# One 64x64-mode stretch per step for the transposed-attention products, x loaded by another queue, and a new head and tail, in a windowed-attention backward kernel

## The chip, the cores and the metric

One core of one Trainium2 chip. The metric is the device time of that core in microseconds (us); the kernel before takes 2076.82 us (median of 3 runs, 2076.24 to 2077.89). Engines: PE (TensorE matmul), PEld (its weight loads), DVE (VectorE), ACT (ScalarE), POOL (GpSimd), SP (the queue that issues most transfers). "SPq" is SP's queue at work issuing.

## The reference

Windowed self-attention with windows of 8x8 pixels on a 256x256 image with 384 channels, and its gradient. All inputs are bfloat16. The outputs are the forward result and the gradients of x, wqkv and wo.

```python
def _fwd_reference(x, wqkv, wo):          # x: 1,256,256,384
    # xw: 1024 windows of 64 tokens x 384
    qkv = xw @ wqkv
    q, k, v = qkv[..., :C], qkv[..., C:2*C], qkv[..., 2*C:]
    p = softmax(einsum('bqc,bkc->bqk', q, k) * C**-0.5)
    o = einsum('bqk,bkc->bqc', p, v) @ wo
    return o                               # back in image order
def reference(x, wqkv, wo, grad_out):
    out, vjp = jax.vjp(_fwd_reference, x, wqkv, wo)
    return (out, *vjp(grad_out))
```

## The kernel before

The kernel handles a "quad" of four 128-row tiles (two windows each) in a step; 128 quads, so 128 full steps and some for filling and draining. It works with the products A = Wq Wk^T and B = Wv Wo and their transposes, so q, k and v are never formed. A step has products that use the whole 128x128 array (projections `proj`, `wgrad`, `outs`, `dxs`) and products on one window's 64 rows (`scores`, `md`, `attn`, `turn_p`). `md` and `attn` run on 64x64 quarters of the array.

All products go to the eight 512-column float32 banks of PSUM (`PS[:, bank, :]`), and DVE or ACT has to empty a bank (`ev`) before the next user writes there. The parts that matter here:

```python
def load(n):                                   # all loads on SP
    for t in range(4):
        SP.dma_start(out=X[...], in_=img(x, n, t))
        SP.dma_start(out=DO[...], in_=img(grad_out, n, t))

def proj(n, a, banks, engs):                   # 128x128 products, 512 columns
    for mo in range(CK):                       # CK = 3
        o = PS[:, banks[mo], :]
        ...                                    # three products each
        ev(engs[mo], YHT[:, n % NYH, a, mo, :], o)

def md(n):                                     # 64x64 quarters
    for m in range(CK):
        ...                                    # 16 products into banks 2m, 2m+1
        for w in range(2):                     # bank 2m by DVE, 2m+1 by ACT, into MD[:, m]
            ev(DVE if w == 0 else ACT, dst, PS[:, 2 * m + w, :]...)

def outs(n, t0, b0, eng):                      # reads MD[:, 0] first
    for i in range(2):
        for m in range(CK):
            mm(PS[:, b0 + i, 0:C], MD[:, m, t0 + i, 2:4, :]..., B_sb[:, m, :], m == 0, m == CK - 1)
    ev(eng, OS[...], PS[:, b0:b0 + 2, 0:C])

def attn(n, t, bvw, bdx): ...                  # 64x64: VW pieces to two banks, dx pieces to a third

def step(n):                                   # T = n, S = n+1, A = n+2
    load(n + 4); turn_in(n + 3)                # turn_in: DMA transposes XT, DOT on SP
    scores(S); chain1(S)                       # chain: softmax and its gradient, DVE/ACT/POOL
    md(T)
    wgrad(g, k0)
    chain2(S); chain3(S)
    outs(T, 0, 0, ACT); outs(T, 2, 2, DVE); outs_st(T)
    proj(A, 0, (4, 5, 0), (ACT, DVE, ACT)); turn_yh(A, 0)
    wgrad(g, k0 + 1)
    attn(T, 0, 2, 4); attn_ev(T, 0, 2, DVE); attn(T, 1, 0, 5); attn_ev(T, 1, 0, ACT)   # 64x64 stretch 1
    dxs(T, 0, 4, ACT); dxs_st(T, 0)
    proj(A, 1, (2, 3, 1), (DVE, ACT, DVE)); turn_yh(A, 1)
    turn_p(S); turn_p_ev(S)
    attn(T, 2, 2, 4); ...; attn(T, 3, 0, 5); ...                                        # 64x64 stretch 2
    dxs(T, 2, 4, ACT); dxs_st(T, 2)
```
(conditions for the first and last steps cut)

Of the kernel before, what the change touches and what calls it, by code (L numbers as in the profile page):

```python
# [16 lines left out]
def kernel(  # L17
# [13 lines left out]
    P = 128  # L31
# [13 lines left out]
    PS = pp.tile([P, 8, 512], F32, name="PS")  # L45
    X = sb.tile([P, NX * 4, C], BF16, name="X")
# [42 lines left out]
    def load(n):  # L89
        for t in range(4):  # L90
            SP.dma_start(out=X[:, (n % NX) * 4 + t, :], in_=img(x, n, t))  # L91
            SP.dma_start(out=DO[:, (n % ND) * 4 + t, :], in_=img(grad_out, n, t))  # L92

    def turn_in(n):
        xs = X[:, (n % NX) * 4:(n % NX) * 4 + 4, :].rearrange("p t c -> p (t c)")
        SP.dma_start_transpose(out=XT[:, n % NXT, :, :], in_=xs)  # L96
        ds = DO[:, (n % ND) * 4:(n % ND) * 4 + 4, :].rearrange("p t c -> p (t c)")
        SP.dma_start_transpose(out=DOT[:, n % NDT, :, :], in_=ds)  # L98
# [5 lines left out]
    def proj(n, a, banks, engs):  # L104
        wgt = A_sb if a == 0 else BT_sb
        src = (XT[:, n % NXT] if a == 0 else DOT[:, n % NDT]).rearrange("p (t m) k -> p m t k", m=CK)
        for mo in range(CK):
            o = PS[:, banks[mo], :]
            for m in range(CK):
                mm(o.rearrange("p (t k) -> p t k", t=4), wgt[:, m, mo * P:(mo + 1) * P], src[:, m, :, :],  # L110
                   m == 0, m == CK - 1)
            ev(engs[mo], YHT[:, n % NYH, a, mo, :], o)
# [31 lines left out]
    def turn_p(n):  # L144
        bb = PS[:, 6, :].bitcast(BF16)
        for t in range(4):
            for a in range(2):
                for w in range(2):
                    r = slice(64 * w, 64 * w + 64)
                    PE.transpose(bb[r, t * P + a * 64:t * P + a * 64 + 64], PB[r, n % 2, a, t, :], ident[r, r])  # L150

    def turn_p_ev(n):
        ev(DVE, TT[:, n % 2].rearrange("p t a k -> p (t a k)"), PS[:, 6, :].bitcast(BF16)[:, 0:512])

    def md(n):
        for m in range(CK):
# [22 lines left out]
    def attn(n, t, bvw, bdx):  # L179
        xs, ds, vw = (n % NX) * 4 + t, (n % ND) * 4 + t, (n % NVW) * 4 + t  # L180
        for a in range(2):
            src = X[:, xs, :] if a == 0 else DO[:, ds, :]
            yh = YH[:, n % NTOK, a, :, :].rearrange("p (m t) k -> p t m k", m=CK)[:, t]
            for cr in range(2):
                for w in range(2):
                    r = slice(64 * w, 64 * w + 64)
                    o = 64 * (w if cr == 0 else 1 - w)
                    if cr == 0:
                        mm(PS[o:o + 64, bvw + a, 0:C], PB[r, n % 2, a, t, :], src[r, :], True, True)
                    else:  # L190
                        mm(PS[o:o + 64, bdx, 0:C].rearrange("p (m k) -> p m k", m=CK), PB[r, n % 2, a, t, :],
                           yh[r], a == 0, False)

    def attn_ev(n, t, bvw, eng):
        ev(eng, VW[:, (n % NVW) * 4 + t, :, :], PS[:, bvw:bvw + 2, 0:C])

    def dxs(n, t0, b0, eng):
        for i in range(2):
            for m in range(CK):
                mm(PS[:, b0 + i, 0:C], MD[:, m, t0 + i, 0:2, :].rearrange("p a k -> p (a k)"), AT_sb[:, m, :],  # L200
                   False, m == CK - 1)
        ev(eng, DXS[:, n % 2, t0:t0 + 2, :], PS[:, b0:b0 + 2, 0:C])
# [6 lines left out]
    def wgrad(g, k):  # L209
# [3 lines left out]
        for i, (q, t) in enumerate(tiles):  # L213
            mm(PS[:, 7, 0:C], X[:, (q % NX) * 4 + t, ma * P:(ma + 1) * P], VW[:, (q % NVW) * 4 + t, which, :],
               i == 0, i == len(tiles) - 1)
        if g == 0:
            DVE.tensor_copy(out=ACC[:, k, :], in_=PS[:, 7, 0:C])
        else:
            DVE.tensor_tensor(out=ACC[:, k, :], in0=PS[:, 7, 0:C], in1=ACC[:, k, :], op=ALU.add)  # L219

    with tc.manual_schedule():

        wT = VW[:].rearrange("p a b c -> p (a b c)")[:, 0:JK * C].rearrange("p (j c) -> p j c", j=JK)
        wo_sb = VW[:].rearrange("p a b c -> p (a b c)")[:, JK * C:(JK + CK) * C].rearrange("p (m c) -> p m c", m=CK)
        for m in range(CK):
            SP.dma_start(out=w_sb[:, m, :], in_=wqkv[m * P:(m + 1) * P, :])
        ACT.dma_start(out=wo_sb[:], in_=wo.rearrange("(m p) n -> p m n", p=P))
        make_identity(nc, ident[:])
        load(0)
        for m in range(CK):  # L230
            SP.dma_start_transpose(out=wT[:, :, m * P:(m + 1) * P], in_=w_sb[:, m, :])  # L231
        for m in range(CK):
            SP.dma_start_transpose(out=woT_sb[:, :, m * P:(m + 1) * P], in_=wo_sb[:, m, :])  # L233
        k = 0
        for dst, lt, r0, sc in ((A_sb, wT[:, 0:CK], wT[:, CK:2 * CK], True),
                                (AT_sb, wT[:, CK:2 * CK], wT[:, 0:CK], True),
                                (B_sb, wT[:, 2 * CK:3 * CK], wo_sb, False),
                                (BT_sb, wo_sb, wT[:, 2 * CK:3 * CK], False)):
            for mo in range(CK):
                o = PS[:, k % 8, 0:C]  # L240
                for m in range(CK):
                    mm(o, lt[:, m, mo * P:(mo + 1) * P], r0[:, m, :], m == 0, m == CK - 1)
                if sc:
                    ACT.activation(out=dst[:, mo, :], in_=o, func=ACTF.Copy, scale=scale)
                else:
                    DVE.tensor_copy(out=dst[:, mo, :], in_=o)
                k += 1

        def step(n):
            T, S, A = n, n + 1, n + 2  # L250
            doT, doS, doA = 0 <= T < NQ, 0 <= S < NQ, 0 <= A < NQ
            g, k0 = n // GQ - 1, 2 * (n % GQ)
            doF = 0 <= g < NG
            if 0 < n + 4 < NQ:
                load(n + 4)
            if 0 <= n + 3 < NQ:
                turn_in(n + 3)
            if doS:
                scores(S)
                chain1(S)  # L260
            if doT:
                md(T)
            if doF:
                wgrad(g, k0)
            if doS:
                chain2(S)
                chain3(S)
            if doT:
                outs(T, 0, 0, ACT)
                outs(T, 2, 2, DVE)  # L270
                outs_st(T)
            if doA:
                proj(A, 0, (4, 5, 0), (ACT, DVE, ACT))
                turn_yh(A, 0)
            if doF:
                wgrad(g, k0 + 1)
            if doT:
                attn(T, 0, 2, 4)
                attn_ev(T, 0, 2, DVE)
                attn(T, 1, 0, 5)  # L280
                attn_ev(T, 1, 0, ACT)
                dxs(T, 0, 4, ACT)
                dxs_st(T, 0)
            if doA:
                proj(A, 1, (2, 3, 1), (DVE, ACT, DVE))
                turn_yh(A, 1)
            if doS:
                turn_p(S)
                turn_p_ev(S)
            if doT:  # L290
                attn(T, 2, 2, 4)
                attn_ev(T, 2, 2, ACT)
                attn(T, 3, 0, 5)
                attn_ev(T, 3, 0, DVE)
                dxs(T, 2, 4, ACT)
                dxs_st(T, 2)

        for n in range(-3, GQ * NG + GQ):
            step(n)


        GF = YHT[:, 0].rearrange("p a m t -> p (a m t)")[:, 0:6 * C].rearrange("p (k c) -> p k c", k=6)
        GFT = YHT[:, 1].rearrange("p a m t -> p (a m t)")[:, 0:6 * C].rearrange("p (k c) -> p k c", k=6)
        for k in range(6):
            ev(DVE if k < 3 else ACT, GF[:, k, :], ACC[:, k, :])
        for h in range(2):
            for mb in range(CK):
# [3 lines left out]
                ev(DVE if h == 0 else ACT, GFT[:, h * CK + mb, :], pt[:, 0:C])  # L311
        dw = VW[:].rearrange("p a b c -> p (a b c)")[:, 0:CK * J].rearrange("p (m j) -> p m j", m=CK)
        dwo = VW[:].rearrange("p a b c -> p (a b c)")[:, CK * J:CK * J + CK * C].rearrange("p (m j) -> p m j", m=CK)
        k = 0
        for ma in range(CK):
            for col, lt, rr, r0 in ((0, GF[:, 0:CK], w_sb, C), (C, GFT[:, 0:CK], w_sb, 0), (2 * C, GFT[:, CK:], woT_sb, 0)):
                o = PS[:, k % 8, 0:C]
                for mb in range(CK):
                    mm(o, lt[:, mb, ma * P:(ma + 1) * P], rr[:, mb, r0:r0 + C], mb == 0, mb == CK - 1)
                if col < 2 * C:  # L320
# [42 lines left out]
```

## Time and profile before

| | before |
|---|---|
| time, median us | 2076.82 |
| span of the profiled run, us | 2072.7 |
| PE busy | 98% |
| first `md` begins at, us | 43.42 |
| usual period of a step, us | 15.66 |
| last `md` to the end, us | 42.7 |

The period is the distance between the starts of successive `md` groups on PE.

From the page of before, two lines: busy times, and the shares in the chain of work that ended last.

```profile
PE 2029.9 (98%) x26970; PEld 1149.4 (55%) x26970; DVE 1358.6 (66%) x2452; ACT 985.1 (48%) x1555; POOL 1012.9 (49%) x1798
...
PE 96%; DMA 2%; SPq 2%; DVE 0%; ACT 0%; issue 0%; DVEq 0%
```

PE is the bound, so a saving has to come out of PE's own sequence. Here is one step of before in PE's timeline (start, length, engine, line, operation, tiles, shapes, count). Matmuls are pipelined and their ends are modelled, so a group's length overlaps the next group: read the distances between starts.

```profile
1015.20 0.95 PE L73 MATMUL PS<-XT,YHT 128*64 128x64 bf16 x48
...
1016.87 2.12 PE L73 MATMUL PS<-VW,X 128*128 128x384 bf16 x12
1018.83 2.11 PE L73 MATMUL PS<-B_sb,MD 128*128 128x384 bf16 x12
1020.78 2.11 PE L73 MATMUL PS<-XT,A_sb 128*128 128x512 bf16 x9
1022.72 2.11 PE L73 MATMUL PS<-VW,X 128*128 128x384 bf16 x12
1024.77 0.35 PE L73 MATMUL PS<-X,PB 64*64 64x384 bf16 x2
...
1029.17 0.33 PE L73 MATMUL PS<-X,PB 64*64 64x384 bf16 x2
1029.49 0.35 PE L73 MATMUL PS<-DO,PB 64*64 64x384 bf16 x2
...
1030.85 0.95 PE L73 MATMUL PS<-XT,YHT 128*64 128x64 bf16 x48
```

The step repeats after 15.65 us (1015.20, 1030.85). Three things are seen. `outs` (B_sb,MD) follows `wgrad` (VW,X) after 1.96 us, which is what twelve products of `wgrad` take. A full-width product group that comes before a 64x64 stretch takes longer to hand over: 1022.72 to 1024.77 is 2.05 us for the same twelve products. And in the second stretch PE goes from 1029.17 to 1029.49, 0.32 us, where one half of a tile takes 0.16. The reason for that gap is in DVE's timeline: DVE is still emptying the bank of the third projection, until 1028.74 + 0.69 = 1029.43.

```profile
1028.74 0.69 DVE L79 CAST YHT<-PS 128x512 bf16<-128x512 f32 x1 [0.67 <-PE PS L73]
```

### The profile page before, as it was taken

How to read it: one execution, taken by the hardware profiler on the slowest of the kernel's cores; microseconds unless marked ns; L12 is line 12 of the kernel's file. 1: busy time of each engine (PE TensorE's matmuls, PEld its weight loads, DVE VectorE, ACT ScalarE, POOL GpSimd, SP SyncE). 2: the span in 40 equal slices, each digit the busy share in tenths (PEclk: the TensorE clock that was granted, in tenths of full speed). 3: DMA queues.
4: the chain of work that ended last, by engine and by line, in shares of the span. 5: the costliest groups of instructions: out<-in, count | busy, mean ns of one | idle time of the engine just before them, and what ended most of it. 6: DMA issues, size and time to landing. Idle time of an engine off the chain costs nothing.

```text
span 2072.7 us, 65934 instructions
## 1 busy us (share of the span) xinstructions
PE 2029.9 (98%) x26970; PEld 1149.4 (55%) x26970; DVE 1358.6 (66%) x2452; ACT 985.1 (48%) x1555; POOL 1012.9 (49%) x1798
## 2 busy tenths in 40 slices
PE   5899999999999999999999999999999999999997
PEld 2455555555555555555555555555555555555554
DVE  3566666666666666666666666666666666666664
ACT  2444444444445444444444444544444444444452
POOL 1454555555555455455555555545545555555552
PEclk9999999999999999999999999999999999999999
DMA  8999999999999999999999999999999999999991
GB/s 177 203 202 202 208 201 197 209 205 198 205 207 200 204 206 200 202 209 198 206 200 205 203 204 203 202 203 205 200 201 208 202 201 204 206 204 200 206 177 56
DMA packets 1030734, 410.90 MB, mean 198 GB/s; under 512 B 865056, under 2 KB 1013280, under 8 KB 1030432
## 3 DMA queue, kind: packets, MB, share of 16 engines
q1 hardware_dynamic: 956304, 305.37, 84.1%
q0 software_dynamic: 73728, 101.02, 18.2%
q8 instruction: 212, 3.47, 0.7%
q14 instruction: 90, 0.74, 0.1%
q10 hardware_dynamic: 400, 0.29, 0.0%
HBM read 101.84 MB, written 101.84 MB: 98 GB/s over the span
## 4 chain that ended last, share of the span: by engine, by line
PE 96%; DMA 2%; SPq 2%; DVE 0%; ACT 0%; issue 0%; DVEq 0%
PE PS L73 94%; PE PS L150 2%; DMA XT<-X 1%; SPq L92 0%; SPq L91 0%; SPq L231 0%; DMA VW<-in_wo_dram 0%; DVE ACC L219 0%; SPq L233 0%; ACT DXS L77 0%; ACT YHT L77 0%; SPq L98 0%; DVE YHT L79 0%; SPq L96 0%; PE PS L310 0%
## 5 line engine op out<-in xcount | busy, mean ns | idle before, releaser
L207 POOL DMA_DIRECT2D out_dram<-DXS x1024 | 572.8, 566 | 583.7 <-ACT DXS L77 561.4
L73 PE MATMUL PS<-VW,X 128*128 128x384 bf16 x3072 | 542.7, 326 | 4.5 <-DVE ACC L219 4.5
L73 PEld LDWEIGHTS <-X 64*64 64x64 bf16 (+1 forms) x9216 | 380.3, 104 | 218.8 <-issue 6.9
L79 DVE CAST YHT<-PS 128x512 bf16<-128x512 f32 x384 | 264.3, 688 | 240.4 <-PE PS L73 238.4
L73 PEld LDWEIGHTS <-MD 128*128 128x128 bf16 x3072 | 279.3, 98 | 232.4 <-issue 61.5
L77 ACT CAST VW<-PS 128x768 bf16<-128x768 f32 x256 | 204.3, 798 | 367.6 <-PE PS L73 367.6
L77 ACT CAST YHT<-PS 128x512 bf16<-128x512 f32 x384 | 224.7, 585 | 277.6 <-PE PS L73 253.7
L219 DVE TENSOR_TENSOR ACC<-PS,ACC 128x384 f32<-128x384 f32 x252 | 140.5, 558 | 257.3 <-PE PS L73 257.3
L73 PE MATMUL PS<-AT_sb,MD 128*128 128x384 bf16 x1536 | 294.1, 328 | 0.0
L141 POOL TENSOR_TENSOR UM<-PB,ST 128x256 f32<-128x256 bf16 x128 | 77.8, 608 | 424.1 <-PE PS L73 367.8
L73 PE MATMUL PS<-XT,A_sb 128*128 128x512 bf16 x1152 | 273.7, 383 | 10.4 <-DMA XT<-X 10.2
L177 POOL DMA_DIRECT2D out_dram<-OS x512 | 276.1, 545 | 13.9 <-issue 11.4
L73 PE MATMUL PS<-B_sb,MD 128*128 128x384 bf16 x1536 | 271.5, 326 | 4.3 <-DVE MD L79 2.5
L73 PE MATMUL PS<-DOT,BT_sb 128*128 128x512 bf16 x1152 | 270.5, 380 | 0.0
L77 ACT CAST DXS<-PS 128x768 bf16<-128x768 f32 x256 | 204.3, 798 | 138.3 <-PE PS L73 138.3
L79 DVE CAST VW<-PS 128x768 bf16<-128x768 f32 x256 | 244.0, 953 | 18.6 <-PE PS L73 4.8
L79 DVE CAST MD<-PS 128x512 bf16<-128x512 f32 x384 | 240.2, 681 | 0.6 <-PE PS L73 0.6
L73 PE MATMUL PS<-YH,PB 64*64 64x384 bf16 x2048 | 238.6, 332 | 1.0 <-ACT DXS L77 1.0
L77 ACT CAST MD<-PS 128x512 bf16<-128x512 f32 x384 | 200.1, 594 | 67.1 <-DVE ST L128 64.6
L77 ACT CAST OS<-PS 128x768 bf16<-128x768 f32 x128 | 102.1, 798 | 194.5 <-PE PS L73 194.5
L73 PEld LDWEIGHTS <-A_sb 128*128 128x128 bf16 x1152 | 113.4, 99 | 135.6 <-issue 12.4
L73 PEld LDWEIGHTS <-BT_sb 128*128 128x128 bf16 x1152 | 113.1, 98 | 123.8 <-issue 2.4
(46 smaller groups left out, 1618.6 us busy)
## 6 DMA issues: line engine op xcount, KB each, us to landing
X<-in_x_dram SPq DMA_DIRECT2D x512, 96.0 KB, 3.1
DO<-in_grad_out_dram SPq DMA_DIRECT2D x512, 96.0 KB, 3.2
out_dram<-OS POOLq DMA_DIRECT2D x512, 96.0 KB, 2.9
out_dram<-DXS POOLq DMA_DIRECT2D x1024, 48.0 KB, 3.8
YH<-YHT SPq DMA_TRANSPOSE x256, 5.4
XT<-X SPq DMA_TRANSPOSE x128, 6.6
DOT<-DO SPq DMA_TRANSPOSE x128, 6.5
w_sb<-in_wqkv_dram SPq DMA_DIRECT2D x3, 288.0 KB, 4.0
```

Of the source, the lines that this page charges most:

```text
L73: PE.matmul(out, lhsT=lhsT, rhs=rhs, start=start, stop=stop, skip_group_check=True)
L77: ACT.copy(out=out, in_=in_)
L79: DVE.tensor_copy(out=out, in_=in_)
L141: POOL.tensor_tensor(out=UM[:], in0=pb[:, 1], in1=bcast(3), op=ALU.mult)
L150: PE.transpose(bb[r, t * P + a * 64:t * P + a * 64 + 64], PB[r, n % 2, a, t, :], ident[r, r])
L177: POOL.dma_start(out=img(out_0, n, t), in_=OS[:, n % 2, t, :])
L207: POOL.dma_start(out=img(out_1, n, t)[8 * w:8 * w + 8], in_=DXS[64 * (1 - w):64 * (1 - w) + 64, n % 2, t, :])
L219: DVE.tensor_tensor(out=ACC[:, k, :], in0=PS[:, 7, 0:C], in1=ACC[:, k, :], op=ALU.add)
```

## The change

Its intent: run all four tiles' `attn` products, and the transposes of P, in one 64x64 stretch, so that the array changes its mode one pair of times less per step. For this, PSUM has to hold the dx sums of four tiles at once: they lie end to end over banks 0 to 2 (tile t at column 384 t), across bank borders, so products are cut where a border falls. The freed bank budget is tight: the third projection's bank is emptied in two halves by ACT and DVE, and `md` takes its blocks in the order 2, 1, 0. Apart from that, x is loaded by POOL's queue and grad_out by SP's, the head transposes wqkv straight from DRAM and brings up the array with empty products, and the tail rotates banks.

```diff
-    def load(n):
-        for t in range(4):
-            SP.dma_start(out=X[:, (n % NX) * 4 + t, :], in_=img(x, n, t))
-            SP.dma_start(out=DO[:, (n % ND) * 4 + t, :], in_=img(grad_out, n, t))
+    def load(n, which):
+        for t in range(4):
+            if which == 0:
+                POOL.dma_start(out=X[:, (n % NX) * 4 + t, :], in_=img(x, n, t))
+            else:
+                SP.dma_start(out=DO[:, (n % ND) * 4 + t, :], in_=img(grad_out, n, t))
@@ proj
-            ev(engs[mo], YHT[:, n % NYH, a, mo, :], o)
+            if engs[mo] is None:
+                ev(ACT, YHT[:, n % NYH, a, mo, 0:256], o[:, 0:256])
+                ev(DVE, YHT[:, n % NYH, a, mo, 256:512], o[:, 256:512])
+            else:
+                ev(engs[mo], YHT[:, n % NYH, a, mo, :], o)
@@ md
-        for m in range(CK):
+        for m in reversed(range(CK)):
@@ attn, dxs
+    def attn_all(n, S):
+        v = (n % NVW) * 4
+        fvw = ((3072, 3584), (1536, 1920), (2304, 2688), (3072, 3584))
+        for t in range(4):
+            attn(n, t, 0, fvw[t][0], t * C)      # products cut at bank borders
+            ...
+            attn(n, t, 1, fvw[t][1], t * C)
+            ...
+        ev(DVE, VW[:, v + 2, :, :]..., PSF[:, 2304:3072])
+        if S is not None:
+            turn_p(S)
+        ...
@@ step
-            proj(A, 0, (4, 5, 0), (ACT, DVE, ACT))
-            turn_yh(A, 0)
         if doF:
             wgrad(g, k0 + 1)
+        if doA:
+            proj(A, 0, (3, 1, 2), (ACT, DVE, None))
+            turn_yh(A, 0)
         if doT:
-            attn(T, 0, 2, 4) ... attn(T, 1, 0, 5) ...
-            dxs(T, 0, 4, ACT)
+            attn_all(T, S if doS else None)
+            dxs(T, 0)
         if doA:
-            proj(A, 1, (2, 3, 1), (DVE, ACT, DVE))
+            proj(A, 1, (3, 4, 5), (ACT, DVE, ACT))
-        if doS: turn_p(S) ...
-        if doT: attn(T, 2, 2, 4) ... attn(T, 3, 0, 5) ... dxs(T, 2, 4, ACT)
+        if doT: dxs(T, 1) ...
@@ head
-            SP.dma_start(out=w_sb[:, m, :], in_=wqkv[m * P:(m + 1) * P, :])
+            SP.dma_start_transpose(out=wT[:, 0:2 * CK, m * P:(m + 1) * P], in_=wqkv[m * P:(m + 1) * P, 0:2 * C])
+        for i in range(14):
+            mm(PS[:, 7, :], wsrc[:, 0:P], wsrc, True, True)
...
+            if n == 2:                           # weights that only the tail needs
+                for m in range(CK):
+                    SP.dma_start(out=w_sb[:, m, :], in_=wqkv[m * P:(m + 1) * P, :])
+                    SP.dma_start_transpose(out=woT_sb[:, :, m * P:(m + 1) * P], in_=wo[m * P:(m + 1) * P, :])
@@ tail (cut): wgrad into banks 3 to 7 in turn, last sums straight to bfloat16, smaller last stores
```

## The prediction

> What bounds it. TensorE. The page gives PE 98% of a 2072.7 us span, and the chain of waits is 96% PE. The timeline's steps repeat every 15.66 us (1015.20, 1030.86). One step, by starts in the timeline: scores 0.88, md 0.79, two wgrad 1.96+2.05, outs 1.95, projections 1.94+2.04, first attention stretch 0.77, dxs 0.99, transposes and second attention stretch 1.21, dxs 1.07. DVE (66%), ACT (48%) and POOL (49%) have slack. SP's queue issues for nearly the whole step (eight loads of 0.6 us, four transposes of 1.8 to 3 us); PE waits 10.2 us for XT in all, nearly all before 100 us.
>
> What the merged stretch removes. A 64x64 group of four products streams in 0.16 us, so a two-tile stretch needs 0.65 us; it took 0.77, and the full-width product before it took 2.05 instead of 1.95. The pair of mode changes thus costs about 0.22 us. This agrees with the Trainium skill, "TensorEngine Tiling (Array Packing)", Key Properties: changing the tiling mode drains TensorE. One pair goes. The second stretch also stalls about 0.16 us for DVE to empty the bank of the third projection (1028.74+0.69, PE restarts at 1029.49). Gain 0.38 to 0.45 us a step.
>
> What it adds. Splits at bank edges: four attention groups and six dxs products more, at about 3 ns each (128-column products ran at 56 ns in the tail): 0.03 us. New waits: with md reversed, DVE empties block 0 last (about 3.7 us after the step's start) and outs needs it first, at 3.63 us: 0.1 to 0.2 us. The third projection's bank is emptied in halves by ACT (estimate 0.37 us) and DVE (0.42 us); tile 2 needs that bank 0.77 us after the stretch begins, and tile 3 needs banks 6 and 7 at about 1.0 us. If the halves run together this costs under 0.1 us, if one waits for the other 0.3 us. So a step of 15.25 to 15.7 us; I take 15.45: 123 full steps save about 26 us.
>
> Queues. x leaves SP: four issues (2.5 us) fewer; POOL gets about 2.2 us more, 10.3 of 15.4 us. The Trainium skill ("DMA: Bandwidth & Descriptors", Issuing engines are not separate DMA queues) says this saves issue time only. It pays in steps 0 to 3 (14.3, 15.6, 18.2, 16.1 us, with waits of 1.4 and 2.4 us for XT): about 4 us.
>
> Head: step 0 begins at 42.55 us; wqkv transposed straight from DRAM, earlier x and warm-up products should bring it to 29 to 34: 11 us. Tail: from the last dxs to the end 30.9 us, of which six waits of 0.65 us plus exposed evictions come from one shared bank; rotating banks, no ACC copies and smaller last stores: about 7 us.
>
> Sum: 26+4+11+7 = 48 us: 2030 us, range 2004 to 2060. Chances: faster by over 2% 0.55, within 2% 0.44, slower 0.01.
>
> To check: step period in the timeline (15.45); 64x64 products in one stretch of about 1.7 to 2.0 us; PE idle before outs released by DVE MD, 0.1 to 0.2 us a step; PE idle in the stretch released by DVE/ACT YHT and VW; no XT waits after the head; first md at about 31 us; tail about 23 us.
>
> What would make it wrong: the halved eviction serialising and the md order together giving back the mode-change gain (step 15.7, total about 2060); no such waits (step 15.25, total about 2004); POOL's stores delaying x, and so XT.

## The result, and the profile after

| | before | after | predicted |
|---|---|---|---|
| time, median us | 2077.34 | 2077.54 | 2030 (2004 to 2060) |
| span of the profiled run, us | 2072.7 | 2076.7 | |
| first `md` begins at, us | 43.42 | 39.20 | 31 |
| usual period of a step, us | 15.66 | 15.745 | 15.45 |
| last `md` to the end, us | 42.7 | 35.8 | about 7 less |

The ratio is 1.0002, with 95% interval 0.9985 to 1.0019 (4 runs each). Ratios here are the mean time of one kernel's fast runs over that of the other's fast runs of the same rounds, so they are not quite the ratio of the medians beside them. A change of hundreds of lines moved the time by nothing. The prediction of 2030 us was wrong by 48 us, which is its whole sum of gains.

Where the time went, by the starts of `md` in the two profiles (differences after minus before):

| stretch | before, us | after, us | difference | predicted |
|---|---|---|---|---|
| start to first `md` | 43.42 | 39.20 | -4.2 | -11 |
| first to sixth `md` | 79.78 | 84.34 | +4.6 | -4 for the queue, and part of the step gain |
| sixth to last `md` | 1906.77 | 1917.39 | +10.6 | -26 |
| last `md` to the end | 42.73 | 35.77 | -7.0 | -7 |
| sum | 2072.7 | 2076.7 | +4.0 | -48 |

(The 4 us between the two profiles are not significant for the times. The first two rows are one profile each: e14 below, the same code up to the tail, has 38.60 and 81.98, so they are good to about 3 us together. The third row is a matter of every step.)

The page after, the same two lines:

```profile
PE 2039.6 (98%) x29800; PEld 1236.2 (60%) x29800; DVE 1342.4 (65%) x2577; ACT 1029.2 (50%) x1810; POOL 1283.0 (62%) x2302
...
PE 96%; DMA 2%; DVE 0%; ACT 0%; SPq 0%; issue 0%; POOL 0%; ACTq 0%
```

By shares nothing has changed: PE 98%, chain 96% PE. The page can't tell this kernel from the other. The timeline of one step on PE can:

```profile
1004.37 0.95 PE L74 MATMUL PS<-XT,YHT 128*64 128x64 bf16 x48
...
1006.05 2.12 PE L74 MATMUL PS<-VW,X 128*128 128x384 bf16 x12
1008.18 2.11 PE L74 MATMUL PS<-B_sb,MD 128*128 128x384 bf16 x12
1010.13 2.11 PE L74 MATMUL PS<-VW,X 128*128 128x384 bf16 x12
1012.08 2.11 PE L74 MATMUL PS<-XT,A_sb 128*128 128x512 bf16 x9
1014.12 0.35 PE L74 MATMUL PS<-X,PB 64*64 64x384 bf16 x2
...
1014.91 0.22 PE L74 MATMUL PS<-X,PB 64*64 64x128 bf16 x2
1015.11 0.24 PE L74 MATMUL PS<-YH,PB 64*64 64x128 bf16 x2
...
1015.33 0.35 PE L74 MATMUL PS<-YH,PB 64*64 64x384 bf16 x2
1015.57 0.35 PE L74 MATMUL PS<-DO,PB 64*64 64x384 bf16 x2
...
1016.11 1.16 PE L74 MATMUL PS<-AT_sb,MD 128*128 128x384 bf16 x9
...
1020.12 0.95 PE L74 MATMUL PS<-XT,YHT 128*64 128x64 bf16 x48
```

The step is 15.75 us here (1004.37, 1020.12), in the mean 15.745. There is one 64x64 stretch now, from 1014.12 to 1016.11. It holds three waits that were not there before:

- `outs`: 1006.05 to 1008.18 is 2.13 us where it was 1.96. 0.17 us.
- In tile 2 of the stretch, at bank 2: the X and YH products of a piece otherwise start within 0.01 us of each other; here YH starts 0.20 us after X (1014.91, 1015.11).
- In tile 3, at bank 7: 1015.33 to 1015.57 is 0.24 us where half a tile takes 0.16. About 0.08 us.

Together 0.45 us, and the stretch was to save 0.38 to 0.45. That is the whole story of the steady part, if the waits are what they seem; the experiments test it.

DVE and ACT after, in the same step, show what ends the waits. First DVE, then ACT:

```profile
1006.16 1.87 DVE L80 CAST MD<-PS 128x512 bf16<-128x512 f32 x3
...
1014.63 0.42 DVE L80 CAST YHT<-PS 128x256 bf16<-128x256 f32 x1 [0.31 <-ACT YHT L78]
1014.97 0.55 DVE L80 CAST VW<-PS 128x384 bf16<-128x384 f32 x1
```

```profile
1005.80 1.56 ACT L78 CAST MD<-PS 128x512 bf16<-128x512 f32 x3 [0.52 <-PE PS L74]
...
1014.23 0.37 ACT L78 CAST YHT<-PS 128x256 bf16<-128x256 f32 x1 [0.71 <-PE PS L74]
```

DVE is done with the last block of `md` at 1006.16 + 1.87 = 1008.03, later than ACT with its part (1005.80 + 1.56 = 1007.36), and `outs`, which needs just that block first, starts at 1008.18. ACT empties its half of the third projection from 1014.23 to 1014.60, and DVE's half does not run beside it but after it: it starts at 1014.63, having waited 0.31 us for ACT, and ends at 1015.05; PE goes on at 1015.11. This happens in every step; the view of waits on DVE counts it 128 times:

```profile
DVE YHT L80 <- ACT YHT L78: 39.7, 128, 0.9
```

The Trainium skill says why a kernel must order them: in "PSUM — Partial Sum Buffer", section "PSUM bank collisions raise a hardware error", accesses of two engines to one bank in the same partitions, reads included, need a semaphore between them. The trace agrees that the two halves are ordered: 0.03 us apart, 128 waits of 0.31 us in the mean. Halves of one bank are thus no parallel work here, while different banks are: in the lines above, DVE and ACT empty the banks of `md` side by side (1006.16 to 1008.03 and 1005.80 to 1007.36).

One trap in reading: the view of PE's waits does not show these stalls. It has for `md`'s block three waits in the whole run:

```profile
PE PS L74 <- DVE MD L80: 6.2, 3, 2.1
```

These three all lie in the first 130 us and last about 2.1 us each, so none of them is the stall of 0.17 us. The modelled end of a matmul group lies about 0.15 us after the next group can start (1018.83 + 2.11 against 1020.78 in before), so a gap of 0.2 us hardly becomes "idle". Distances between starts show it; idle times don't. The Trainium skill warns of it ("Perfetto Trace Analysis", section "Tensor Engine Instruction (MATMUL, LD_WEIGHTS)"): the end reported for a TensorE instruction is computed, not observed. The 0.17 us before `outs`, in every later step and in none of the view's three waits, is what that amounts to here.

The head. Lines of before, then of after, from the start (SPq and ACTq are queues issuing):

```profile
7.50 4.32 SPq L231 DMA_TRANSPOSE VW<-w_sb  x3
...
13.97 8.56 PE L73 MATMUL PS<-VW 128*128 128x384 bf16 x36 [13.97 <-DMA VW<-w_sb]
```

```profile
0.74 4.04 SPq L326 DMA_TRANSPOSE VW<-in_wqkv_dram  x3
...
13.74 3.04 PE L74 MATMUL PS<-VW 128*128 128x384 bf16 x9 [7.72 <-DMA DO<-in_grad_out_dram]
```

The transposes of wqkv are issued 6.8 us earlier than before, but the first weight product begins at 13.74 instead of 13.97. The waiting line names grad_out's load, yet the chain of work that ended last names the transposes of wqkv from DRAM: 10.11 us from 3.50 to just before that product. The three landed 4.3, 7.6 and 10.1 us after their issue, where the transposes from SBUF of before took 3.4 to 3.7; loads of x (four of them on POOL from 1.51 us on), wo and grad_out were under way beside them. The experiments on the head below show what x on POOL has to do with it. The second weight product then waits another 3.8 us for the last third of wqkv, whose transposes SP issued only from 15.08 us on. Nor do the empty products show a gain: after them PE stood idle for 7.72 us, and three weight products then took 0.96 us, as in before (ACT's evictions begin at 14.89, 15.85, 16.81 here and at 15.12, 16.09, 17.05 there).

### The profile page after: what moved, and what is told of

Its sections match the earlier page's. It is cut to its first block, busy times and chain, and to the rows that moved or that the text cites. A ratio compares the mean times of both kernels' runs of the same rounds, so it can differ in the third digit from the quotient of the medians.

```text
span 2076.7 us, 72109 instructions
## 1 busy us (share of the span) xinstructions
PE 2039.6 (98%) x29800; PEld 1236.2 (60%) x29800; DVE 1342.4 (65%) x2577; ACT 1029.2 (50%) x1810; POOL 1283.0 (62%) x2302
## 4 chain that ended last, share of the span: by engine, by line
PE 96%; DMA 2%; DVE 0%; ACT 0%; SPq 0%; issue 0%; POOL 0%; ACTq 0%
PE PS L74 95%; PE PS L157 2%; DMA XT<-X 1%; DMA VW<-in_wqkv_dram 1%; DMA X<-in_x_dram 0%; DMA out_dram<-DXS 0%; DVE MD L80 0%; ACT DXS L78 0%; ACT VW L372 0%; SPq L335 0%; SPq L326 0%; POOL X L93 0%; DVE OS L80 0%; SPq L99 0%; DVE ACC L255 0%
## 5 line engine op out<-in xcount | busy, mean ns | idle before, releaser
L78 ACT CAST YHT<-PS 128x512 bf16<-128x512 f32 (+1 forms) x512 | 273.2, 534 | 539.4 <-PE PS L74 539.4
L74 PEld LDWEIGHTS <-MD 128*128 128x128 bf16 x3840 | 329.7, 98 | 214.4 <-issue 48.1
L80 DVE CAST YHT<-PS 128x512 bf16<-128x512 f32 (+1 forms) x384 | 231.3, 602 | 263.5 <-PE PS L74 223.7
L74 PE MATMUL PS<-AT_sb,MD 128*128 128x384 bf16 (+2 forms) x2304 | 294.7, 273 | 1.8 <-ACT DXS L78 1.8
L93 POOL DMA_DIRECT2D X<-in_x_dram x504 | 270.7, 555 | 33.2 <-DMA out_dram<-DXS 19.8
L80 DVE CAST VW<-PS 128x384 bf16<-128x384 f32 (+1 forms) x384 | 252.1, 684 | 55.9 <-PE PS L74 52.6
L78 ACT CAST VW<-PS 128x384 bf16<-128x384 f32 (+1 forms) x384 | 224.3, 585 | 43.6 <-PE PS L157 21.7
L74 PE MATMUL PS<-YH,PB 64*64 64x256 bf16 (+2 forms) x3072 | 226.8, 274 | 0.0
L74 PEld LDWEIGHTS <-PB 64*64 64x64 bf16 x6144 | 143.2, 106 | 112.3 <-issue 100.4
L134 DVE TENSOR_REDUCE ST<-PS 128x4 f32<-128x256 f32 x128 | 54.3, 424 | 231.8 <-PE PS L74 231.8
```

The lines of the kernel that those rows point to most:

```text
L74: PE.matmul(out, lhsT=lhsT, rhs=rhs, start=start, stop=stop, skip_group_check=True)
L78: ACT.copy(out=out, in_=in_)
L80: DVE.tensor_copy(out=out, in_=in_)
L93: POOL.dma_start(out=X[:, (n % NX) * 4 + t, :], in_=img(x, n, t))
L134: DVE.tensor_reduce(out=ST[:, 0, :], in_=ps_sd(0), axis=AX.X, op=ALU.max)
```

## The experiments

Sixteen kernels ran; all gave correct results. Every one is timed against the kernel before on the same chip. "Period" is the mean over steps 20 to 120 unless said otherwise.

| run | what | median us | ratio to before (95%) | period us |
|---|---|---|---|---|
| after | the change | 2077.54 | 1.0002 (0.9985 to 1.0019) | 15.745 |
| e1_md_fwd | after, `md` order forward | 2065.22 | 0.9947 (0.9928 to 0.9966) | 15.648 |
| e2_outs_rev | after, `outs` takes blocks in `md`'s order | 2054.46 | 0.9898 (0.9883 to 0.9913) | 15.570 |
| e3_third_dve | after, third projection emptied by DVE alone | 2060.91 | 0.9933 (0.9918 to 0.9948) | 15.609 |
| e4_x_on_sp | after, x back on SP | 2150.66 | 1.0366 (1.0350 to 1.0381) | 16.35 |
| e5_mode_pair | before, one more mode pair | 2106.46 | 1.0141 (1.0126 to 1.0156) | 15.910 |
| e6_mode_none | before, control for e5 | 2084.07 | 1.0034 (1.0019 to 1.0049) | 15.717 |
| e7_split | before, 12 products cut | 2083.03 | 1.0022 (1.0005 to 1.0038) | 15.69 (median) |
| e8_w_spread | after, tail's weights loaded apart | 2077.69 | 0.9997 (0.9983 to 1.0012) | as after |
| e9_waits_gone | after, two waits taken away | 2033.32 | 0.9798 (0.9781 to 0.9814) | 15.37 (median) |
| e10_all | e9 and e8 | 2027.76 | 0.9760 (0.9746 to 0.9775) | 15.370 |
| e11_before_x_pool | before, x on POOL | 2065.09 | 0.9946 (0.9930 to 0.9963) | 15.660 |
| e12_waits_gone_x_sp | e9, x back on SP | 2139.70 | 1.0308 (1.0283 to 1.0334) | 16.23 |
| e13_old_head | after, head of before | 2073.15 | 0.9980 (0.9965 to 0.9994) | 15.747 |
| e14_old_tail | after, tail of before | 2084.52 | 1.0043 (1.0027 to 1.0059) | 15.746 |
| e15_x_sp_inter | e12, loads in before's order | 2135.94 | 1.0284 (1.0249 to 1.0319) | 16.21 |
| e16_best | e9 with head of before | 2023.26 | 0.9746 (0.9731 to 0.9760) | 15.375 |

My theory after the result was "waits": the merged stretch gains what was foretold, and three new waits give it back. Rivals: the mode change costs less than 0.2 us, so there was nothing to gain; the cut products cost more than a few ns; and POOL's queue, now with x, delays something.

### Is a mode pair worth anything? e5_mode_pair and e6_mode_none

To the kernel before, one tiny 64x64 transpose is added between two full-width groups, so the array changes to the 64x64 mode and back once more. The control adds a 128x128 transpose at the same place, with no change of mode.

```diff
                 outs(T, 2, 2, DVE)
+                if doA:
+                    PE.transpose(PS[:, 4, :].bitcast(BF16)[0:64, 0:64], ident[0:64, 0:64], ident[0:64, 0:64])
# e6_mode_none instead:
+                    PE.transpose(PS[:, 4, :].bitcast(BF16)[:, 0:128], ident[:], ident[:])
```

> The kernel before, with one 64x64 transpose (64 columns) put between outs and the projection of x in 126 of the 128 steps, so that each of these steps has one more change into the 64x64 mode and back; its result is overwritten. If a pair of mode changes costs 0.22 us, as read from the trace, the step grows by 0.22 to 0.27 us, total about 2077 + 28 to 34 = 2105 to 2111 us. If the pair is free and the gaps were something else: about 2080 us.

> Control of the run before: the same place, but a 128x128 transpose (128 columns), so no change of mode. One such product took 56 ns in the tail: 126 x 0.056 = 7 us, total about 2084 us, whatever the mode change costs.

Measured: 15.910 and 15.717 us a step, against 15.66. PE's timeline in e5, and after it in e6, from `outs` over the added product to the projection:

```profile
1003.52 2.11 PE L73 MATMUL PS<-B_sb,MD 128*128 128x384 bf16 x12
1005.56 0.21 PE L272 MATMUL PS<-ident 64*64 64x64 bf16 x1
1005.71 2.12 PE L73 MATMUL PS<-XT,A_sb 128*128 128x512 bf16 x9
```

```profile
1103.45 2.11 PE L73 MATMUL PS<-B_sb,MD 128*128 128x384 bf16 x12
1105.40 0.22 PE L272 MATMUL PS<-ident 128*128 128x128 bf16 x1
1105.45 2.11 PE L73 MATMUL PS<-XT,A_sb 128*128 128x512 bf16 x9
```

From `outs` to the projection it is 2.19 us with the pair of changes and 2.00 without: 0.19 us, of which 0.09 going in and 0.10 coming out. The Trainium skill, "TensorEngine Tiling (Array Packing)", Key Properties, says that changing the tiling mode drains TensorE; this is the figure for it here. (The control's product has 128 columns and the added one 64, so the pair may cost up to 0.03 us more, an estimate from half of the 0.057 us that e6 adds to a step.) The prediction's 0.22 holds nearly, and the rival "mode change is free" falls.

### Do the cut products cost much? e7_split

In the kernel before, all twelve `dxs` products of a step are cut in 128 + 256 columns.

```diff
-                mm(PS[:, b0 + i, 0:C], MD[:, m, t0 + i, 0:2, :]..., AT_sb[:, m, :], False, m == CK - 1)
+                for c0, c1 in ((0, P), (P, C)):
+                    mm(PS[:, b0 + i, c0:c1], MD[:, m, t0 + i, 0:2, :]..., AT_sb[:, m, c0:c1], False, m == CK - 1)
```

> The kernel before, with all twelve dxs products of a step cut into 128 and 256 columns (twice the cuts that the change makes there; twelve more products and weight loads a step). Theory W: about 3 ns each, 0.04 us a step, total about 2082 us. Rival S: 25 ns or more each, 0.3 us a step, total 2115 us or more.

Measured: the usual period is 15.69, so 0.03 us for twelve cuts, 2 to 3 ns each; a few single steps were longer, which makes the mean 15.709. The change has fewer cuts in `dxs` (six), so this rival falls for them. The cut attention products were not tested alone; e9 below leaves little room for a cost of theirs.

### The wait before outs: e1_md_fwd and e2_outs_rev

Two ways to take the same wait away. e1 undoes the reversed `md`. e2 keeps it and makes `outs` follow it, blocks 2, 1, 0, with the first pair of tiles in banks 4 and 5, which are emptied first.

```diff
# e1_md_fwd
-        for m in reversed(range(CK)):
+        for m in range(CK):
# e2_outs_rev
-            for m in range(CK):
-                mm(PS[:, b0 + i, 0:C], ..., m == 0, m == CK - 1)
+            for m in reversed(range(CK)):
+                mm(PS[:, b0 + i, 0:C], ..., m == CK - 1, m == 0)
-            outs(T, 0, 0, ACT)
+            outs(T, 0, 4, ACT)
```

> The kernel after with md's blocks in their old order (0, 1, 2). Theory W: the 0.17 us before outs goes, but md's first blocks now need banks 1 and 2, which ACT is still emptying of dxs (until about 1.0 us after the scores begin, md begins at 0.88): 0.1 to 0.2 us of wait there instead. Step 15.6 to 15.8 us, total 2060 to 2083 us; if the wait at md is really as short as 0.1 us, the reversed order cost more than it saved.

> The kernel after, with one wait taken away: outs takes the three MD blocks in the order in which md now finishes them (2, 1, 0), and its first two tiles go to banks 4 and 5, which md frees first. Theory W (the merged stretch does gain about 0.38 us a step, and three new PE waits of 0.17, 0.20 and 0.09 us spend it): the 0.17 us between the end of wgrad and the start of outs goes, step 15.745 to about 15.57 us, total about 2056 us. Rival S (the pieces at bank edges, with their extra products and weight loads, cost the gain): no change, 2077 us. Rival Q (x on POOL's queue, and the transfers' contention, cost the gain): no change.

Measured: e2 has 15.570 us a step, 0.175 less than the change, which is the wait of 0.17 read from the starts, and in its timeline `outs` follows `wgrad` after 1.96 us:

```profile
1008.05 2.12 PE L74 MATMUL PS<-VW,X 128*128 128x384 bf16 x12
1010.01 2.11 PE L74 MATMUL PS<-B_sb,MD 128*128 128x384 bf16 x12
```

The total fell by 23 us. e1 has 15.648: the wait before `outs` is gone there too, but `md` now takes 0.88 us instead of 0.79, because its first block needs a bank that ACT has yet to empty of `dxs`. So the reversed order was put in for a good reason (about 0.09 us), it cost twice that, and reversing `outs` as well has both.

### The halved eviction: e3_third_dve

```diff
-            proj(A, 0, (3, 1, 2), (ACT, DVE, None))
+            proj(A, 0, (3, 1, 2), (ACT, DVE, DVE))
```

> The kernel after, with the third projection block emptied whole by DVE instead of in halves by ACT and then DVE. Theory W: the halves run one after the other (in the trace DVE starts 0.03 us after ACT ends) and hold bank 2 until 0.93 us after the stretch begins; one whole block on DVE (0.69 us) frees it at about 0.8 us. The stretch with its transposes shrinks from 1.99 us to about 1.8 us, of which the wait for bank 7 may take back 0.05: step about 15.6 us, total about 2058 to 2065 us. Rivals S and Q: no change, 2077 us.

Measured: 15.609 us, 0.136 less than the change. The wait in tile 2 is 0.06 us, where it was 0.20:

```profile
1005.33 0.22 PE L74 MATMUL PS<-X,PB 64*64 64x128 bf16 x2
1005.39 0.24 PE L74 MATMUL PS<-YH,PB 64*64 64x128 bf16 x2
```

One engine that empties the whole bank (0.69 us for 512 columns) is done sooner than two that take turns (0.37 + 0.03 + 0.42, after ACT's later start). That the two halves serialise cost the change 0.14 us a step; the rest of the wait, the bank being needed early, remains in e3 (0.06 us).

### Both waits away: e9_waits_gone

e2's edits, and the first projection before the second `wgrad`, so that there are 1.95 us of other work between the projection's last product and the stretch that reuses its banks. With that room ACT can empty the third bank alone.

```diff
# e2's edits, and
-        if doF:
-            wgrad(g, k0 + 1)
         if doA:
-            proj(A, 0, (3, 1, 2), (ACT, DVE, None))
+            proj(A, 0, (0, 1, 4), (ACT, DVE, ACT))
             turn_yh(A, 0)
+        if doF:
+            wgrad(g, k0 + 1, 5)
```

> The kernel after without the three new waits: outs in md's order as in the first run, and the projection of x moved ahead of the second wgrad (as it stood before the change), its blocks in banks 0, 1 and 4, each emptied whole by one engine, and that wgrad in bank 5. All that the merged stretch reads or writes stays. Theory W: the step falls to 15.24 to 15.35 us, total 2016 to 2032 us. Rival S: the step stays above 15.6 us, total above 2060 us. Rival Q: likewise.

Measured: 2033.32 us, usual period 15.37 (the mean is 15.383, as four steps were longer), just above what was expected. One step of it on PE:

```profile
1000.07 2.12 PE L74 MATMUL PS<-VW,X 128*128 128x384 bf16 x12
1002.03 2.11 PE L74 MATMUL PS<-B_sb,MD 128*128 128x384 bf16 x12
...
1007.96 0.35 PE L74 MATMUL PS<-X,PB 64*64 64x384 bf16 x2
...
1009.75 1.16 PE L74 MATMUL PS<-AT_sb,MD 128*128 128x384 bf16 x9
```

`outs` comes 1.96 us after `wgrad`, and the stretch takes 1.79 us (1007.96 to 1009.75) instead of 1.99. So the change's 15.745 less 0.17 less 0.20 is 15.37: the two waits read from the timeline account for the difference to within 0.01 us. The merged stretch alone, without them, is worth 15.66 - 15.37 = 0.29 us a step, with the wait at bank 7 still in it (the expectation spoke of three waits; the edit takes two away).

### Was POOL's queue the hindrance? e4_x_on_sp, e11_before_x_pool, e12_waits_gone_x_sp, e15_x_sp_inter

e4 puts x back on SP in the change; e11 puts it on POOL in the kernel before; e12 is e9 with x on SP; e15 is e12 with x and grad_out loads alternating as before had them.

```diff
# e4_x_on_sp, and e12_waits_gone_x_sp on top of e9
-                POOL.dma_start(out=X[:, (n % NX) * 4 + t, :], in_=img(x, n, t))
+                SP.dma_start(out=X[:, (n % NX) * 4 + t, :], in_=img(x, n, t))
# e11_before_x_pool (kernel before)
-            SP.dma_start(out=X[:, (n % NX) * 4 + t, :], in_=img(x, n, t))
+            POOL.dma_start(out=X[:, (n % NX) * 4 + t, :], in_=img(x, n, t))
# e15_x_sp_inter: as e12, and each x load followed at once by the grad_out load of the same tile
```

> The kernel after, with x loaded by SP's queue again. Theory W: the step stays at 15.745 us, as PE waits for no transfer in mid-run; only the first five steps can get longer, total 2077 to 2090 us. Rival Q: the step falls back by 0.1 us or more and the total to about 2060 us.

> The kernel before, with only x's loads moved to POOL's queue. PE waits for no transfer in mid-run there, so the step stays at 15.66 us; only the first steps can gain: 2068 to 2078 us. If relief of SP's queue is worth something by itself in mid-run: below 2065 us.

> The version without the three waits (2033.3 us), with x back on SP's queue. The change with x on SP took 2150.7 us, with PE waiting for XT in half of the steps. Theory O (order): that loss comes from the projection of x standing after the second wgrad, which makes SP's queue wait longer for YHT; here the projection stands early again, so the total is about 2033 to 2045 us. Theory L (load): SP's queue has about 16 us of issue a step, so any step shorter than about 15.7 us is bound by it: the step is 15.7 to 16.6 us, total 2080 to 2150 us.

> The version without the three waits and with x on SP's queue (2139.7 us), but with the loads of x and grad issued alternately, as the kernel before did, instead of four of x and then four of grad. If the order of the loads makes the difference (the kernel before kept a step of 15.66 us with the same twelve issues): step 15.4 to 15.7 us, total 2040 to 2080 us. If the number of issues alone binds: no change, step about 16.2 us, total 2130 to 2150 us.

Measured: I was wrong in e4 by 60 us and more. It took 2150.66 us; its steps range from 15.74 to 19.87 us, and PE waits for transposed x, which in before it did in the first steps only. The lines of PE's waits for XT, before and then e4:

```profile
PE PS L73 <- DMA XT<-X: 10.2, 5, 3.5
```

```profile
PE PS L74 <- DMA XT<-X: 59.3, 50, 3.8
```

In e11 the middle of the run is as before (15.660), and yet the total falls by 11 us: the first five steps take 13.97, 14.09, 14.48, 15.75, 15.66 us in place of 14.27, 15.55, 18.16, 16.14, 15.66, and the first `md` begins at 38.29 us in place of 43.42. (The total of 2065.09 lies just outside both expectations, 2068 to 2078 and below 2065.) So POOL's queue is not a hindrance but a gain over head and ramp, nearly three times the 4 us of the prediction, and in the changed kernel it is a condition: without it 73 us are lost.

I had thought that the order of the projection (after `wgrad` in the change) made x's transposes late in e4. e12, with the projection early again, loses as much (period 16.23), and e15, with the loads alternating, too (16.21). Both thoughts fall. What came in are the other expectations of these two runs, that SP's queue has no room (15.7 to 16.6 us a step, and about 16.2).

SP's trace agrees with them. Summed issue by issue over steps 20 to 120, in us a step:

| kernel | period | SP issuing | SP in pauses over 0.3 us |
|---|---|---|---|
| before (x on SP) | 15.66 | 14.7 | 0.06 |
| e4, e12, e15 (x on SP) | 16.35, 16.23, 16.21 | 15.4, 15.3, 15.2 | 0.06 |
| e11 (before, x on POOL) | 15.66 | 13.0 | 2.0 |
| the change (x on POOL) | 15.75 | 12.1 | 3.0 |
| e9 (x on POOL) | 15.38 | 12.6 | 2.1 |

With x on SP its queue never pauses, in before either; so before, as far as the trace tells, already ran without room there. e9 against e12, which differ by x's queue alone, shows what a shorter step then needs: 15.38 us with x on POOL, 16.23 with x on SP. Two things stay open. The same twelve issues take 14.7 us a step in before and 15.2 to 15.4 in the three others; an issue's length may contain waiting, which the trace does not set apart. And moving x changes more than who issues: in e11 the run has 981585 DMA packets instead of 1030734, and the DMA engines are busy at 90% or more in nearly every slice of the pages before and after; no run varies that load alone. The time from issue to landing of x's transposes does not explain the loss (median 6.7 us before, 6.2 in e12, from 400 to 1600 us).

The Trainium skill, "DMA: Bandwidth & Descriptors", section "Issuing engines are not separate DMA queues", says that issuing from several engines saves only the time of issuing, which is usually small. e11's steady steps agree (15.660 against 15.66). In its ramp, and in e4, the differences are 11 and 73 us, which is not small; how much of them is time of issuing no run here sets apart.

### Head and tail: e13_old_head, e14_old_tail, e8_w_spread

e13 gives the change the head of before, with x on POOL; this also takes away the weight loads after step 2. e14 gives it the tail of before. e8 keeps the change but loads the weights that the tail needs at steps 20, 40 and 60 instead of all after step 2.

```diff
# e8_w_spread
-            if n == 2:
-                for m in range(CK):
+            if n in (20, 40, 60):
+                m = n // 20 - 1
# e13_old_head: head of before, cut;  "for n in range(-3, NQ): step(n)", no weight loads later
# e14_old_tail: tail of before, cut;  "for n in range(-1, GQ * NG + GQ): step(n)"
```

> The kernel after, with the head of the kernel before (weights loaded first and transposed from SBUF, no warm-up products, all four weight products before the first step, no weight loads after step 2); steps and tail as after. Theory R (the first ten steps are paced by the transfers, so a head that starts the steps sooner only makes them wait): total within 4 us of the kernel after, 2074 to 2082 us. Rival H (the head as such saved the 4 us by which the first md starts sooner, and the weight loads after step 2 lost 5): total 2074 us or less, with no step over 17 us. If the new head is worth what was predicted: 2086 us or more.

> The kernel after with the tail of the kernel before (one shared bank for the last weight gradients, copies of ACC, one large store). In the traces the stretch from the last md to the end took 42.7 us before and 35.8 us after. If that is the tail's doing: total about 2077.5 + 6 to 8 = 2083 to 2086 us. If the gain is only moved from the waits of the last steps: under 2080 us.

> The kernel after, with the loads and transposes of the weights that only the tail needs issued in three steps far apart (20, 40 and 60) instead of all at the end of step 2. The trace of after shows a step of 20.71 us just after them, in which PE waits 3.4 us for XT. If the six issues on SP's queue (6.4 us) cause it, the step falls to about 15.75 us and the total by about 5 us, to 2072 us. If x on POOL's queue (which was waiting for a store to land) causes it: no change, 2077 us.

Measured: e14 is 7 us slower than the change, so the new tail is worth just what was predicted. e13 is 4 us faster than the change by the medians, but the intervals of the ratio overlap, and it meets neither theory in full (2073.15 us, yet one step of 17.78). e16 against e9 (below), which differ by the head and its later weight loads alone, makes it clear: with these, the new head costs about 10 us (2023.26 against 2033.32, intervals that do not overlap).

In e13 the first `md` starts at 38.30 us and in the change at 39.20, and the next five steps take 80.8 and 84.3 us. Over all the profiles, by head and by x's queue (the steps differ too, so the last column mixes):

| head, x's queue | runs | first weight product, us | first `md`, us | sixth `md`, us |
|---|---|---|---|---|
| old, SP | before, e5 to e7 | 13.9 to 14.4 | 41.9 to 43.6 | 123.2 to 127.3 |
| old, POOL | e11, e13, e16 | 16.3 to 17.9 | 38.3 to 38.6 | 112.2 to 119.1 |
| new, SP | e4, e12, e15 | 10.2 to 10.7 | 35.8 to 36.3 | 127.0 to 132.6 |
| new, POOL | the change and the rest | 12.5 to 13.7 | 37.5 to 39.2 | 117.2 to 123.5 |

Like for like, the new head brings the first weight product forward by about 3 to 5 us, and x on POOL delays it by 2 to 4. To the first `md`, with x on SP the new head gains about 6 to 8 us; with x on POOL nothing that shows. The two gains do not add, and by the sixth `md` nothing of the new head's is left. What holds up the steps there is not settled. The granted clock may have a part: over the first 20 us it is 0.78 in the change and 1.00 in before, e11, e13 and e16 (from 20 to 40 us 0.87 in the change, 0.83 in before and 1.00 in e13); no run sets this apart.

In the change, one step of 20.71 us stands out, the fifth. PE waits in it for the transpose of x, which SP issued behind the six weight transfers (issued from 97.99 to 104.4 us):

```profile
113.21 3.53 PE L74 MATMUL PS<-XT,A_sb 128*128 128x512 bf16 x9 [3.39 <-DMA XT<-X]
```

In e8's profile that step is gone and the profiled run took 2071.96 us, 6 us less than the change's median. But its other three runs took 2077.19 to 2078.25. So e8 alone is inconclusive. That the weight loads make the long step isn't shown either: e2, e3 and e14 issue the same loads at the same place, and their fifth step takes 15.57 to 15.75 us; in these the first step is the long one (18.8 to 21.6 us, 17.5 in the change).

### Together: e10_all and e16_best

e10 is e9 with e8's loads (5 rounds); e16 is e9's edits on e13's head.

```diff
# e10_all = e9_waits_gone + e8_w_spread
# e16_best = e9_waits_gone + e13_old_head
```

> The version without the three waits, with the tail's weights loaded in three steps far apart as well. The version without the waits gave 2033.3 us. If the early 5 us are really saved by spreading the loads: about 2028 us. If, as the unprofiled runs of the spreading alone suggest (2072 to 2078 us), the lost time only moves to another early step: 2031 to 2035 us.

> The version without the three waits, with the head of the kernel before. The old head made the kernel after 4.4 us faster; if that holds here too: 2033.3 - 4.4, about 2029 us, and not clearly different from the version with spread weight loads (2027.8 us). Step 15.37 us.

Measured: e10 2027.76 us, below e9's 2033.32, with intervals of the ratio that don't overlap (0.9746 to 0.9775 against 0.9781 to 0.9814); so on top of e9 spreading the weights did pay, though on the change itself it had not. The two were run on different chips, and I leave that contradiction as it is. e16 is 2023.26 us, 2.5% faster than before and than the change; it is the best version found. I had expected about 2029 us; against e10 the intervals overlap, as expected. Its parts: steps of 15.37, the head of before with x on POOL (first `md` at 38.55), and the new tail.

## Why the prediction was wrong

**"64x64 mode pair about 0.22 us; gain 0.38 to 0.45 us a step": nearly right.** The pair costs 0.19 us (e5 against e6), and the DVE stall of the old second stretch was 0.16. With the waits gone the step is 15.37, so 0.29 us net of the cuts and of the wait at bank 7; 0.29 + 0.03 + 0.08 is 0.40 (an estimate, with the 0.03 of e7 for the cuts); the two parts measured apart, 0.19 + 0.16, come to 0.35.

**"So a step of 15.25 to 15.7 us; I take 15.45": this is the step that failed.** The mechanisms were both named: `outs` waiting for the block that DVE empties last, and the halved bank. The term for them was mis-sized. The sum behind 15.45 gives them about 0.2 us; they measured 0.17 + 0.20 + 0.08 = 0.45. I had myself written 0.1 to 0.2 us for the first and 0.3 for the second "if one waits for the other", which come to 0.4 to 0.5, and then took the favourable case without asking whether the two halves of one bank would be emptied at once. They take turns: 128 waits in the run, and e3 shows that this turn-taking alone costs 0.14 us a step. The step came out 0.295 us longer than I took, which on about 123 steps is 36 us of the 48.

**"Head: 29 to 34 us; 11 us": wrong.** I took the issue time of the direct transposes (earlier by 6.8 us) as a measure of when the data lands. In the change the first weight product began only 0.23 us earlier than before; with x on SP it began 3.4 us earlier (10.55, e4). The transposes landed 4.3 to 10.1 us after issue, beside x's first loads, which the change had moved to POOL. The missing step is this time from issue to landing of a transpose from DRAM, which the trace of before has nowhere, because it does not do it; I should have called that term unknown. And I added a gain of the head and one of the queue that do not add: to the first `md` each alone gains (7.1 us in e4, 5.1 in e11), both together 4.2. By the sixth `md` the new head has lost what it gained.

**"About 4 us" for the queue: too small, and its role misread.** It gave 11 us to the kernel before (e11), and taking it back costs the changed kernel 73 us (e4). The prediction read SP's queue as issuing for nearly the whole step and still gave it weight in steps 0 to 3 only; in e4, e12 and e15 that queue has no pauses, and in e4 PE waits 50 times for x's transposes.

**"Tail about 7 us": right** (7 us in e14, 7.0 in the profile).

**"Range 2004 to 2060; what would make it wrong: step 15.7, total about 2060": the cause was the one I named,** but the total was 17 us worse than my bad case, because that case kept the head's 11 us and 4 us of the ramp, of which the profile shows +0.3 us to the sixth `md`.

**Checks that misled.** I had named "PE idle released by DVE MD, 0.1 to 0.2 us a step" as the sign. The stall is there and of that size, but the view of idle times shows none of it (its three waits belong to the first 130 us). Starts of groups were the right thing to look at.

## What to carry to other kernels

When a merge takes away a fixed cost of 0.2 us, list the bank reuses that move closer together, and for each compare when the emptying engine ends with when PE arrives; three that are late by 0.1 to 0.2 us undo it. Splitting the eviction of one bank over two engines bought no parallelism here (0.82 us against 0.69); put other work between producer and reuse instead, and let the reader take its pieces in the order in which they are emptied. Time a new head apart from the old one with everything else equal: here the two parts that each brought the first `md` forward did not add. And before you shorten a step, look whether the queue that issues its transfers ever pauses: here it did not, and x had to leave it.

## What the Trainium skill lacked or had wrong

- "TensorEngine Tiling (Array Packing)", Key Properties: it says that a mode change drains TensorE but has no figure. Here a pair of changes between 128x128 and 64x64 cost 0.19 us (15.910 against 15.717 us a step).
- "PSUM — Partial Sum Buffer", section "PSUM bank collisions raise a hardware error": right, but it could say what follows for tuning: half a bank by ACT and half by DVE took 0.82 us from start to end, and one whole bank by DVE 0.69 us.
- "DMA: Bandwidth & Descriptors", section "Issuing engines are not separate DMA queues": "usually small" is no guide for a queue without room. SP issued for 14.7 us of a step of 15.66; moving four loads a step left the steady step as it was (e11, 15.660) but gave 11 us over head and ramp, and in the changed kernel, with its own step, it was worth 73 us. That all of this is time of issuing is not shown.
- The same page, section "Latency and other measured facts", gives 261 GB/s as the effective bandwidth of a DMA transpose, or more. An estimate from it for 768 columns of wqkv (384 x 768 x 2 bytes, 590 KB) is 2.3 us. Here these three transposes from DRAM were issued from 0.74 to 4.8 us and landed 4.3, 7.6 and 10.1 us after their issue, with loads of x, wo and grad_out in flight beside them. What the page lacks is the time beside other transfers.
- Why the same twelve issues take SP 15.2 to 15.4 us a step in the changed kernels with x on it, and 14.7 in the kernel before, no run here tells, and I found no page that does.
